# Two raw token tiles in the first wave: layer-norm folded into the PSUM correction of a fused MLP kernel

## The chip, the cores and the metric

The kernel runs on one core of one Trainium2 chip. The metric is device time in microseconds (us) of one execution; lower is better. The number given for a kernel is the median of its runs. Engines are called by the profile's names: PE is TensorE, DVE is VectorE, ACT is ScalarE, POOL is GpSimd, SP is SyncE, which here only starts transfers.

## The reference

A layer-norm without gain or offset, a linear layer with GELU, and a second linear layer, all in bfloat16:

```python
B, S, D, F = 1, 2048, 1024, 3584

def reference(x, w1, b1, w2, b2):
    y = _layernorm(x, axis=-1)               # (x - mean) / sqrt(var + 1e-5)
    h = _gelu(jnp.einsum("bsd,df->bsf", y, w1) + b1)
    return jnp.einsum("bsf,fd->bsd", h, w2) + b2
```

## The kernel before

**Tiling.** The 2048 tokens are 16 tiles of 128 tokens, four tiles to a block of 512. For a block, the first product makes 28 rows (F is 28 x 128). A row is one PSUM bank of 128 x 512 and takes 8 matmuls over the 8 slices `dt` of D; ACT then reads it with GELU and `b1` into `hT_sb` (L432). The second product follows tile by tile, 28 matmuls to a bank (L466); DVE adds `b2` (L477) and SP stores (L482). Blocks run one after another on PE.

**Transposes.** The first product needs x transposed, in `yT_sb` (two buffers, by block number). For blocks 1 to 3 DVE does it out of the PE's way (L355). For block 0 PE does it: `pe_T` (L367) puts 128 x 128 transposes into a PSUM bank and ACT copies them out to `yT_sb` (L385). Tiles 1 to 3 use one bank, `ps_t`, in two groups of four transposes each, so a second group waits until the copy of the first is done.

**The first wave.** As data come in piece by piece, the first 7 rows of block 0 (r = 0 to 6) are not computed 512 tokens at a time but in cells of one tile, one row and one slice: 4 x 7 x 8 = 224 matmuls of 128 columns, in a hand-written order (L508 to L522) in which the transposes of tiles 1 to 3 are inserted at the places of `T_PUTS`. Seven PSUM banks are open at once: five of `ps_1` and two of `ps_2`. Row 7 is the first of full width; it uses `ps_t`, row 8 the bank of row 0, and so on, so row 8 + j waits for the GELU of row j.

**Layer-norm.** DVE takes statistics of a tile in two halves (L264), joins them (L271), POOL raises the variance to the power -0.5 (L268), and DVE normalises (L290). For tiles 0 and 1 only the mean is taken off before the transpose (tile 0 by a mean got early, half of it by ACT, L494; tile 1 at L286). Their factor 1/deviation is put on after the first product: DVE spreads it over the partitions with 16 small transposes (L337), and multiplies columns 0 to 255 of every row of block 0 in PSUM by it before the GELU (`dve_scale`, L423 to L428).

**Order.** Each engine runs its own list in order; a waiting instruction holds all behind it. PE starts with 34 warm-up matmuls on constants, 3 more that wait for tile 0's mean, and 3 after the first transposes (L490). ACT starts the loads of the second half of tile 0 and of tile 1, SP all others: the 8 chunks of w1 that the wave needs (224 KB each, one for each slice), then tiles 2 and 3, `b1`, the rest of w1, x of block 1, w2. DVE's work of later blocks is merged by a small planner (L569 to L584) that only sets the order.

Of the kernel before, what the change touches and what calls it, by code (L numbers as in the profile page):

```python
# [5 lines left out]
ACT = mybir.ActivationFunctionType  # L6
# [5 lines left out]
P = 128  # L12
# [3 lines left out]
K_GROUPS = 2  # L16
# [4 lines left out]
WARM_A = ((34, None), (3, "m4"))  # L21
WARM_B = 3
N_CENTRED = 2
T_PUTS = {0: (None, None, 6), 1: (21, 35), 2: (96, 118), 3: (140, 156)}
NORM = {0: (0, 2, 8), 1: (0, 4, 8), 2: (0, 4, 8)}
GROUPS_0 = (0, 2, 5, 8)
WAVE_ROWS_0 = 6
WAVE_K = (0, 2, 4, 5, 6, 8)
GROUPS_1 = (0, 4, 8)
W1_CHUNK_COLS = (512, 512, 1024, 640)  # L30
N_W2_CHUNKS = 4
SP_FIRST_LOADS = ("x0a", "w0", "w1", "w2", "w3", "w4", "w5", "x2a", "x2b", "w6", "w7", "x3a", "x3b", "b1", "w8")
ACT_FIRST_LOADS = ("x0b", "x1")

T_PE_START = 5.7
T_DVE_START = 16.5
# [54 lines left out]
def bass_standalone__mixer_channel_mlp__prompt_kernel(  # L91
# [22 lines left out]
    nkg = max(1, min(K_GROUPS, DT))  # L114
    KGROUPS = [(h * DT // nkg, (h + 1) * DT // nkg) for h in range(nkg)]
    assert NB1 + NB2 + 1 <= 8 and NB2 == 2
    assert all(c[-1] == DT for c in (*NORM.values(), GROUPS_0, GROUPS_1, WAVE_K))
# [27 lines left out]
    with ExitStack() as es:  # L145
# [19 lines left out]
        half_sb = sb("half_sb", [P, 1], F32)  # L165
        m4_sb = sb("m4_sb", [P, 1], F32)
        rq_sb = sb("rq_sb", [P, N_CENTRED, 32], F32)
        rbc_sb = sb("rbc_sb", [P, N_CENTRED, P], F32)

# [4 lines left out]
        ps_tf = ps_t[:, :, :].bitcast(F32)  # L174

# [83 lines left out]
        pool.op(lambda e: e.memset(b1r_sb[:, :], 0.0), sig="b1z")  # L259
        dve.op(lambda e: e.memset(st_sb[:, :, 12:14], 0.0))  # L260
# [6 lines left out]
        def op_aggr(i):  # L267
            pool.op(lambda e, i=i: e.tensor_tensor(out=rstd_sb[:, i:i + 1], in0=mv_sb[:, i, 1:2],  # L268
                                                   in1=nhalf[:, i:i + 1], op=ALU.pow),
                    waits=[f"mv{i}", "nhalf"], sig=f"rstd{i}")  # L270
            return (lambda e, i=i: e.bn_aggr(mv_sb[:, i, :], st_sb[:, i, :]),  # L271
                    [f"st{i}_0", f"st{i}_1", "eps"], f"mv{i}", 0.33)

        def op_mean0():
            return (lambda e: e.tensor_scalar(out=m4_sb[:, :], in0=st_sb[:, 0, 1:2], scalar1=st_sb[:, 0, 4:5],
                                              scalar2=half_sb[:, :], op0=ALU.add, op1=ALU.add),
                    ["st0_0", "half"], "m4", 0.1)

        def op_norm(i, c0, c1, sig):
            if i == 0:  # L280
                return (lambda e, c0=c0, c1=c1: e.tensor_scalar(
                            out=o_sb[:, 0, c0:c1], in0=x_sb[:, 0, c0:c1], scalar1=4.0,
                            scalar2=m4_sb[:, :], op0=ALU.mult, op1=ALU.subtract),
                        ["m4"], sig, 0.02 + (c1 - c0) * 0.00055)
            if i < N_CENTRED:
                return (lambda e, i=i, c0=c0, c1=c1: e.tensor_scalar(  # L286
                            out=x_sb[:, i, c0:c1], in0=x_sb[:, i, c0:c1], scalar1=mv_sb[:, i, 0:1],
                            scalar2=None, op0=ALU.subtract),
                        [f"mv{i}"], sig, 0.02 + (c1 - c0) * 0.00055)
            return (lambda e, i=i, c0=c0, c1=c1: e.tensor_scalar(  # L290
                        out=x_sb[:, i, c0:c1], in0=x_sb[:, i, c0:c1], scalar1=mv_sb[:, i, 0:1],
                        scalar2=rstd_sb[:, i:i + 1], op0=ALU.subtract, op1=ALU.mult),
                    [f"rstd{i}", f"mv{i}"], sig, 0.02 + (c1 - c0) * 0.00055)
# [3 lines left out]
        def ops_norm(i):  # L297
            cuts = NORM.get(i, (0, DT))
# [27 lines left out]
        def ops_rbc():  # L326
            res = []
            for i in range(N_CENTRED):
                res.append((lambda e, i=i: e.tensor_scalar(out=rq_sb[:, i, :], in0=ones[:, 0:32],
                                                           scalar1=rstd_sb[:, i:i + 1], scalar2=(1.0 if i else 0.25),  # L330
                                                           op0=ALU.mult, op1=ALU.mult),
                            ["ones", f"rstd{i}"], f"rq{i}", 0.1))
            for tq in range(4):
                for q in range(4):
                    src = rq_sb[32 * tq:32 * (tq + 1), :, :]
                    dst = rbc_sb[32 * q:32 * (q + 1), :, 32 * tq:32 * (tq + 1)]
                    res.append((lambda e, src=src, dst=dst: e.transpose(out=dst, in_=src), [f"rq{N_CENTRED - 1}"],  # L337
                                ("rbc" if tq == 3 and q == 3 else None), 0.1))
            return res
# [4 lines left out]
        def ops_T(i):  # L344
            blk, t = divmod(i, TPB)
            waits = [y_ev[i][-1]]
            if blk - 2 in mm1_done:
                waits.append(mm1_done[blk - 2])
            res = []
# [15 lines left out]
        t_banks = [("t", ps_t[:, 0, :]), ("2_0", ps_2b[:, 0, :]), ("t", ps_t[:, 0, :])]  # L365

        def pe_T(i, groups, k):  # L367
            blk, t = divmod(i, TPB)
            j0, j1 = groups[k], groups[k + 1]
            bname, bap = t_banks[k if i == 0 else 0]  # L370
            evs = yT_ev.setdefault(i, [None] * DT)
            for j in range(j0, j1):
# [3 lines left out]
                if j == j0 or y_ev[i][j] != y_ev[i][j - 1]:  # L376
                    waits.append(y_ev[i][j])
                pe.op(lambda e, i=i, j=j, o=(j - j0) * P, bap=bap: e.transpose(  # L378
                    out=bap[:, o:o + P], in_=(x_sb[:, i] if i else o_sb[:, 0])[:, j * P:(j + 1) * P],
                    identity=ident[:, :]),  # L380
# [3 lines left out]
            dst = yT_sb[:, blk % 2, j0:j1, t * P:(t + 1) * P]  # L384
# [23 lines left out]
        def pe_cell(b, r, t0, t1, bank, waits, sig, dts=None, opens=True, closes=True):  # L408
            n0, n1 = t0 * P, t1 * P
            dts = list(range(DT)) if dts is None else list(dts)  # L410
            waits = list(waits)
            for k, dt in enumerate(dts):
                w = (waits if k == 0 else []) + [f"w1c{w1_chunk_of(r, dt)}"]
                w += [yT_ev[b * TPB + t][dt] for t in range(t0, t1)]
                pe.op(lambda e, b=b, r=r, dt=dt, n0=n0, n1=n1, bank=bank: e.matmul(  # L415
                    unit_bank(bank)[:, n0:n1], lhsT=w1_sb[:, dt, r * P:(r + 1) * P], rhs=yT_sb[:, b % 2, dt, n0:n1],
                    start=(opens and dt == 0), stop=(closes and dt == DT - 1)),
                    waits=w, sig=(sig if dt == DT - 1 else None))
            pe_t[0] += len(dts) * _mm_us(n1 - n0)
            if dts[-1] == DT - 1:  # L420
                est[sig] = pe_t[0]

        def dve_scale(r, bank, wait_ev):  # L423
            ap = unit_bank(bank)[:, 0:N_CENTRED * P]
            crit.append((est[wait_ev], (lambda e, ap=ap: e.tensor_tensor(  # L425
                out=ap, in0=ap, in1=rbc_sb[:, :, :].rearrange("p t s -> p (t s)"), op=ALU.mult),
                [wait_ev, "rbc"], f"sc_{r}", 0.35), 0))
            return f"sc_{r}"  # L428
# [11 lines left out]
        def mm1_row(b, r):  # L440
            bank, uw = new_unit()
            sig = f"m1_{b}_{r}"
            pe_cell(b, r, 0, TPB, bank, uw, sig)
            act_gelu(r, 0, TPB, bank, dve_scale(r, bank, sig) if b == 0 else sig, f"g_{b}_{r}")
# [8 lines left out]
        def out_chunk(b, st, c0, c1, region, prev_store):  # L453
# [9 lines left out]
            else:  # L463
                waits.append(bank_gelu[("2", bank)])
            for ft in range(FT):
                pe.op(lambda e, st=st, ft=ft, c0=c0, c1=c1, bank=bank: e.matmul(  # L466
# [21 lines left out]
        def warm(n, gate=None):  # L488
            for _ in range(n):
# [4 lines left out]
        act.op(lambda e: e.activation(out=o_sb[:, 1, 0:HC], in_=x_sb[:, 0, HC:D], func=ACT.Copy, scale=2.0 / HC,  # L494
                                      accum_out=half_sb[:, :]), waits=[x_ev[0][1]], sig="half")
        for n, gate in WARM_A:
            warm(n, gate)
        head = [op_stats(0, 0), op_mean0()] + ops_norm(0) + ln_seq([1], ()) + [op_stats(0, 1), op_aggr(0)]
        for o in head + ln_seq(list(range(2, TPB)), ()) + ops_b1() + ops_rbc():
            dve_put(o)  # L500

        for k in range(2):
            pe_T(0, GROUPS_0, k)
        warm(WARM_B)
        wave = [new_unit() for _ in range(R)]
        r5 = min(R, WAVE_ROWS_0)
        _, ka, kb, kc, kd, _ = WAVE_K
        order = [(0, r, dt) for dt in range(ka) for r in range(r5)]  # L508
        order += [(0, r, dt) for r in range(r5, R) for dt in range(ka)]
        order += [(0, r, dt) for dt in range(ka, kc) for r in range(R)]  # L510
        order += [(1, r, dt) for r in range(R) for dt in range(kb)]
        order += [(0, r, dt) for dt in range(kc, kd) for r in range(R)]
        order += [(1, r, dt) for r in range(R) for dt in range(kb, kd)]
# [114 lines left out]
```

## Time and profile before

| | |
|---|---|
| median of 3 runs | 398.56 us (398.50 to 398.64) |
| span of the profiled execution | 396.9 us |
| PE busy | 394.1 us, 99% of the span |
| DVE, ACT, POOL busy | 152.8, 82.8, 9.7 us |
| L415, first product, all matmuls | 167.4 us (`ps`) and 34.0 us (`ps_t`) |
| L466, second product | 194.2 us |
| DMA | busy in the first 55 us, then near nothing |

The profile is of one execution. Its span, first to last instruction, is 396.9 us; the device time counts what lies around it too, and the median is 1.66 us above the span. A row of the page's groups gives the line, the engine and operation, output and input tiles with their shapes, the count, then busy time, mean duration of one in ns, and idle time of the engine just before them with what ended it. PE's matmuls overlap: a 128-column matmul lasts 219 ns in the records but follows the one before by 56 ns.

### The profile page before, as it was taken

Reading aid. Unit: us, or ns where it says so; the run is one execution under the profiler, and the core shown is the slowest. Engines: PE = TensorE matmul, PEld = TensorE weight load, DVE = VectorE, ACT = ScalarE, POOL = GpSimd, SP = SyncE. Lnnn points to the kernel's source line nnn. Section 1 sums busy time; section 2 is a strip of 40 time slices with the busy share of each in tenths; the row PEclk is TensorE's granted clock in tenths of the full one; section 3 lists DMA queues with packets and bytes.
Section 4 is the critical chain, followed back from the end, with each engine's and each line's share of the span. In section 5 each row is a group of like instructions: output and inputs, shape, how many; then the busy total and the mean of one; then the engine's idle time right before and its main releaser. Section 6 shows DMA issues by size and latency. Waiting matters only on the chain.

```text
span 396.9 us, 4883 instructions
## 1 busy us (share of the span) xinstructions
PE 394.1 (99%) x2116; PEld 191.7 (48%) x2116; DVE 152.8 (38%) x345; ACT 82.8 (21%) x124; POOL 9.7 (2%) x24
## 2 busy tenths in 40 slices
PE   9999999999999999999999999999999999999998
PEld 8944444444444444444444444444444444444447
DVE  5847899989998005988100000001100000001011
ACT  4273430000133442000024433100003334400000
POOL 2101000020002000000000000000000000000000
PEclk9999999999999999999999999999999999999999
DMA  8999940000000000000000000000000000000000
GB/s 286 347 380 384 387 154 13 26 29 13 26 2 0 2 0 1 28 13 26 28 13 0 2 0 2 13 13 28 16 24 15 0 0 2 0 13 28 13 28 26
DMA packets 16924, 23.64 MB, mean 60 GB/s; under 512 B 1672, under 2 KB 10504, under 8 KB 16904
## 3 DMA queue, kind: packets, MB, share of 16 engines
q1 hardware_dynamic: 16616, 22.95, 16.4%
q8 instruction: 16, 0.26, 0.3%
q10 hardware_dynamic: 288, 0.39, 0.3%
q14 instruction: 4, 0.03, 0.0%
HBM read 19.14 MB, written 4.19 MB: 59 GB/s over the span
## 4 chain that ended last, share of the span: by engine, by line
PE 99%; ACT 0%; DVE 0%; issue 0%
PE ps L466 49%; PE ps L415 41%; PE ps_t L415 8%; PE ps L490 1%; PE ps_t L378 0%; ACT yT_sb L385 0%; DVE o_sb L477 0%
## 5 line engine op out<-in xcount | busy, mean ns | idle before, releaser
L466 PE MATMUL ps<-w_sb,hT_sb 128*128 128x512 bf16 (+1 forms) x980 | 194.2, 361 | 0.0
L415 PE MATMUL ps<-yT_sb,w_sb 128*128 128x512 bf16 (+1 forms) x920 | 167.4, 340 | 0.1
L466 PEld LDWEIGHTS ps<-w_sb,hT_sb 128*128 128x128 bf16 x980 | 91.3, 98 | 102.7
L415 PEld LDWEIGHTS ps<-yT_sb,w_sb 128*128 128x128 bf16 x920 | 80.9, 98 | 82.5 <-issue 0.3
L432 ACT ACTIVATE hT_sb<-ps,b_sb 128x512 bf16<-128x512 f32 x94 | 64.0, 688 | 237.2 <-PE ps L415 217.1
L477 DVE TENSOR_TENSOR o_sb<-ps,b_sb 128x512 bf16<-128x512 f32 (+1 forms) x35 | 22.6, 646 | 198.2 <-PE ps L466 198.1
L355 DVE STREAM_TRANSPOSE yT_sb<-x_sb 32x256 bf16<-32x256 bf16 x192 | 83.7, 436 | 26.6 <-PE ps_t L415 23.5
L415 PE MATMUL ps_t<-yT_sb,w_sb 128*128 128x512 bf16 x144 | 34.0, 379 | 0.0
L264 DVE BATCH_NORM_STATS2 st_sb<-x_sb 128x6 f32<-128x512 bf16 x32 | 21.1, 674 | 4.9 <-DMA x_sb<-in_x_dram 4.9
L415 PEld LDWEIGHTS ps_t<-yT_sb,w_sb 128*128 128x128 bf16 x144 | 14.0, 98 | 16.8
L432 ACT ACTIVATE hT_sb<-ps_t,b_sb 128x512 bf16<-128x512 f32 x18 | 12.4, 690 | 17.0 <-PE ps_t L415 14.6
L425 DVE TENSOR_TENSOR ps<-ps,rbc_sb 128x256 f32<-128x256 f32 x24 | 9.7, 426 | 6.1 <-PE ps L415 5.9
L268 POOL TENSOR_TENSOR rstd_sb<-mv_sb,nhalf 128x1 f32<-128x1 f32 x16 | 8.9, 559 | 118.7 <-DVE mv_sb L271 118.7
L290 DVE TENSOR_SCALAR x_sb<-x_sb,mv_sb,rstd_sb 128x1024 bf16<-128x1024 bf16 (+1 forms) x15 | 7.8, 525 | 3.9 <-POOL rstd_sb L268 3.3
L385 ACT COPY yT_sb<-ps_t 128x512 bf16<-128x512 bf16 (+2 forms) x8 | 4.4, 545 | 8.1 <-PE ps_t L378 8.1
L490 PE MATMUL ps<-const-bfloat16-1.0 128*128 128x128 bf16 x40 | 4.6, 302 | 0.8 <-PEq L613 0.8
L490 PEld LDWEIGHTS ps<-const-bfloat16-1.0 128*128 128x128 bf16 x40 | 4.0, 139 | 1.0 <-issue 0.8
L271 DVE BATCH_NORM_AGGREGATE mv_sb<-st_sb 128x2 f32<-128x15 f32 x16 | 3.5, 221 | 1.3
L337 DVE STREAM_TRANSPOSE rbc_sb<-rq_sb 32x64 f32<-32x64 f32 x16 | 3.8, 236 | 0.2
L378 PE MATMUL ps_t<-ident,x_sb 128*128 128x128 bf16 x24 | 2.3, 219 | 0.0
L425 DVE TENSOR_TENSOR ps_t<-ps_t,rbc_sb 128x256 f32<-128x256 f32 x4 | 1.6, 405 | 0.1
L493 ACT ACT_TABLE_LOAD x1 | 1.3, 1283 | 1.7 <-PEq L613 1.7
(24 smaller groups left out, 8.0 us busy)
## 6 DMA issues: line engine op xcount, KB each, us to landing
w_sb<-in_w_dram SPq DMA_DIRECT2D x4, 1792.0 KB, 18.3
out_dram<-o_sb SPq DMA_DIRECT2D x31, 128.0 KB, 1.7
x_sb<-in_x_dram SPq DMA_DIRECT2D x3, 1024.0 KB, 14.1
w_sb<-in_w_dram SPq DMA_DIRECT2D x2, 1024.0 KB, 9.1
w_sb<-in_w_dram SPq DMA_DIRECT2D x1, 2048.0 KB, 15.2
w_sb<-in_w_dram SPq DMA_DIRECT2D x8, 224.0 KB, 4.7
w_sb<-in_w_dram SPq DMA_DIRECT2D x1, 1280.0 KB, 14.7
x_sb<-in_x_dram SPq DMA_DIRECT2D x5, 128.0 KB, 4.6
```

The source lines that it names most:

```text
L264: return (lambda e, i=i, h=h: e.bn_stats(st_sb[:, i, 6 * h:6 * (h + 1)], x_sb[:, i, h * HC:(h + 1) * HC]), [x_ev[i][h]], f"st{i}_{h}", 0.65)
L268: pool.op(lambda e, i=i: e.tensor_tensor(out=rstd_sb[:, i:i + 1], in0=mv_sb[:, i, 1:2], in1=nhalf[:, i:i + 1], op=ALU.pow), waits=[f"mv{i} ...
L290: return (lambda e, i=i, c0=c0, c1=c1: e.tensor_scalar(out=x_sb[:, i, c0:c1], in0=x_sb[:, i, c0:c1], scalar1=mv_sb[:, i, 0:1], scalar2=rst ...
L337: res.append((lambda e, src=src, dst=dst: e.transpose(out=dst, in_=src), [f"rq{N_CENTRED - 1}"], ("rbc" if tq == 3 and q == 3 else None), ...
L355: res.append((lambda e, src=src, dst=dst: e.transpose(out=dst, in_=src), waits, (f"tr{i}" if lastop else None), 0.47))
L385: act.op(lambda e, dst=dst, src=src: e.copy(out=dst, in_=src), waits=[f"tp{i}_{k}"], sig=f"te{i}_{k}")
L415: pe.op(lambda e, b=b, r=r, dt=dt, n0=n0, n1=n1, bank=bank: e.matmul(unit_bank(bank)[:, n0:n1], lhsT=w1_sb[:, dt, r * P:(r + 1) * P], rhs= ...
L425: crit.append((est[wait_ev], (lambda e, ap=ap: e.tensor_tensor(out=ap, in0=ap, in1=rbc_sb[:, :, :].rearrange("p t s -> p (t s)"), op=ALU.m ...
L432: act.op(lambda e, r=r, n0=n0, n1=n1, bank=bank: e.activation(out=hT_sb[:, r, n0:n1], in_=unit_bank(bank)[:, n0:n1], func=ACT.Gelu_apprx_tanh,
L466: pe.op(lambda e, st=st, ft=ft, c0=c0, c1=c1, bank=bank: e.matmul(ps_2[:, bank, 0:c1 - c0], lhsT=hT_sb[:, ft, st * P:(st + 1) * P], rhs=w2 ...
L477: crit.append((est[sig], (lambda e, ob=ob, c0=c0, c1=c1, bank=bank: e.tensor_tensor(out=o_sb[:, ob, c0:c1], in0=ps_2[:, bank, 0:c1 - c0], ...
L490: pe.op(lambda e: e.matmul(ps_1[:, 0, 0:P], lhsT=unit, rhs=unit, start=True, stop=True), waits=[gate] if gate else [])
```

## The change

Tiles 0 and 1 are transposed as they are loaded, with neither mean nor deviation applied, into buffer 1 of `yT_sb`: tile 1 in columns 0 to 127, tile 0 in 128 to 255 (`SLOT_0`). Column 256 of that buffer is set to one. A wave cell of tiles 0 and 1 together has 257 columns (of tile 0 alone 129), so PSUM column 256 of each row gathers the sum of its weights over D. ACT copies these sums out (`act_cs`), and the cells of tile 2, which lie on columns 256 to 383, then add onto that column.

When a row of the wave is complete, DVE multiplies columns 0 to 256 by a row vector that holds 1/deviation of each token (and 1), and adds the weight sum times a second row vector that holds -mean/deviation (and -1, which takes the sum off column 256 again). The two vectors are made by DVE as columns, turned by four 32 x 32 transposes, stored by ACT's queue to device memory (2 KB) and loaded back to all 128 partitions (256 KB), the second transfer waiting for the first on ACT. For rows 7 on, DVE makes normalised tiles 0 and 1 in buffer 0 of `yT_sb` from the raw ones with the same vectors (`ops_fix`, four operations on 128 x 1024), so the scaling of rows 7 to 27 in PSUM goes. Row 7 is done in two halves, tiles 2 and 3 first.

Tile 1's load moves from ACT's queue to third place on SP's. There are 24 warm-up matmuls, and none after. The transposes of tiles 2 and 3 stand at new places in the wave, which has 28 cells of 128 or 129 columns for tiles 0 and 1, 42 of 257, and 112 of 128 for tiles 2 and 3. Rows 8 to 27, blocks 1 to 3, the second product and the stores keep their instructions.

```diff
-WARM_A = ((34, None), (3, "m4"))
-WARM_B = 3
+WARM = 24
+N_RAW = 2
+RC = N_RAW * P
+SLOT_0 = (1, 0, 2, 3)
-SP_FIRST_LOADS = ("x0a", "w0", "w1", "w2", "w3", "w4", "w5", "x2a", "x2b", "w6", "w7", "x3a", "x3b", "b1", "w8")
-ACT_FIRST_LOADS = ("x0b", "x1")
+SP_FIRST_LOADS = ("x0a", "w0", "x1", "w1", "w2", "w3", "x2a", "x2b", "w4", "w5", "w6", "w7", "x3a", "x3b", "b1", "w8")
+ACT_FIRST_LOADS = ("x0b",)
...
+        pool.op(lambda e: e.memset(yT_sb[:, 1, :, RC:RC + 1], 1.0), sig="rone")
...
+        def op_nmr(i):
+            return (lambda e, i=i: e.tensor_scalar(out=nmr_ap[i], in0=mv_sb[:, i, 0:1], scalar1=rstd_ap[i],
+                                                   scalar2=-1.0, op0=ALU.mult, op1=ALU.mult),
+                    [f"rstd{i}", f"mv{i}"], f"nmr{i}", 0.1)
+        def ops_rvt():
+            return [(lambda e, q=q: e.transpose(out=rvt_sb[:, 32 * q:32 * (q + 1)], in_=rv_sb[32 * q:32 * (q + 1), :]),
+                     ["nmr0", "nmr1"], ("rvt" if q == 3 else None), 0.18) for q in range(4)]
...
+        def ops_fix(i):
+            s0, s1 = SLOT_0[i] * P, (SLOT_0[i] + 1) * P
+            return [(lambda e: e.tensor_tensor(out=tmp_sb, in0=yT_sb[:, 1, :, s0:s1], in1=row_bc(0, s0, s1),
+                                               op=ALU.mult),
+                     ["rows", f"te{i}_{len(GROUPS_1) - 2}", f"te{i}_0"] + ([f"fx{i + 1}"] if i == 0 else []), f"fm{i}", 1.1),
+                    (lambda e: e.tensor_tensor(out=yT_sb[:, 0, :, s0:s1], in0=tmp_sb, in1=row_bc(1, s0, s1),
+                                               op=ALU.add),
+                     [f"fm{i}"], f"fx{i}", 1.1)]
...
-        for o in head + ln_seq(list(range(2, TPB)), ()) + ops_b1() + ops_rbc():
+        for o in ln_seq([0], ()) + ln_seq([1], ()) + [op_nmr(0), op_nmr(1)] + ops_rvt() + ln_seq([2], ()):
             dve_put(o)
...
+        for o in stats3 + ops_b1() + norm3 + ops_fix(1) + ops_fix(0):
+            dve_put(o)
...
+        def act_cs(banks, r0, r1, flip):
+            src = banks[:, :, RC]
+            act.op(lambda e: e.copy(out=cs_sb[:, r0:r1], in_=src), waits=[f"cw_{r}" for r in range(r0, r1)],
+                   sig=f"cs_{r0}")
...
+        def ops_corr(r):
+            ap = unit_bank(wave[r][0])[:, 0:RC + 1]
+            return [(lambda e: e.tensor_tensor(out=ap, in0=ap, in1=row_sb[:, 0, :], op=ALU.mult),
+                     [f"m1_0_{r}", "rows", "row1"], f"sa_{r}", 0.43),
+                    (lambda e: e.scalar_tensor_tensor(out=ap, in0=row_sb[:, 1, :], scalar=cs_ap[r], in1=ap,
+                                                      op0=ALU.mult, op1=ALU.add),
+                     [f"sa_{r}", cs_ev[r]], f"sb_{r}", 0.43)]
+
+        pe_T(0, 0, "t")
+        pe_T(0, 1, "2_0")
+        t0_cells(range(r5), (0,))
+        pe_T(1, 0, "t")
+        t0_cells(range(r5), (1,))
+        pe_T(1, 1, "2_0")
+        act.op(lambda e: e.dma_start(rows_d, rvt_sb[0:2 * N_RAW, :]), waits=["rvt"],
+               sig="rvd", sem="d_rvd", inc=16)
+        act.op(lambda e: e.dma_start(row_sb[:, :, 0:RC],
+                                     rows_d.rearrange("(k t) s -> k (t s)", k=2).partition_broadcast(P)),
+               waits=["rvd", "row1"], sig="rows", sem="d_rows", inc=16)
+        t1_cells(range(r5), (0, 1))
+        raw_both(range(r5), (2,))
+        t0_cells(range(r5, R), (0, 1))
+        t1_cells(range(r5, R), (0, 1))
+        raw_both(range(r5, R), (2,))
+        raw_both(range(R), range(3, DT - 1))
+        pe_T(2, 0, "t")
+        raw_both(range(NB1), (DT - 1,))
+        act_cs(ps_1, 0, NB1, False)
+        raw_both(range(NB1, R), (DT - 1,))
+        act_cs(ps_2, NB1, R, True)
+        pe_T(2, 1, "t")
+        h = DT // 2
+        wave_cells(2, range(R), range(h))
+        wave_cells(2, range(4), range(h, DT))
+        pe_T(3, 0, "t")
+        wave_cells(2, range(4, R), range(h, DT))
+        r4 = R // 2 + 1
+        wave_cells(3, range(2), range(h))
+        pe_T(3, 1, "t")
+        wave_cells(3, range(2, r4), range(h))
+        wave_cells(3, range(r4), range(h, DT))
+        wave_cells(3, range(r4, R), range(DT))
+        for o in corr:
+            dve_put(o)
...
-                mm1_row(b, r)
+                mm1_row(b, r, ((TPB // 2, TPB), (0, TPB // 2)) if b == 0 and r == r0 else ((0, TPB),))
```

## The prediction

> **What bounds the kernel now.** I read the chain that ended last first: it is PE from end to end.
>
> ```profile
> PE 99%; ACT 0%; DVE 0%; issue 0%
> ```
>
> So only what moves PE's stream counts, and the change touches its first 20 us alone. The same chain, cut to the first 22 us (start, length, what; x is the number of instructions), shows that stretch:
>
> ```profile
> 0.82 4.26 PE ps L490 x37
> 5.08 0.30 PE ps_t L378 x2
> 5.38 0.02 issue
> 5.40 0.38 ACT yT_sb L385
> 5.78 0.14 issue
> 5.92 0.49 PE ps L415 x6
> ...
> 16.37 3.80 PE ps L415 x68
> ```
>
> The wave's first cell starts at 5.92, after warm-up, two transposes and their copy. In the groups by shape of the first 20 us, the cells have no idle time to speak of:
>
> ```profile
> L415 PE MATMUL ps<-yT_sb,w_sb 128*128 128x128 bf16 x224 | 13.9, 219 | 0.1
> ```
>
> The timeline of PE and ACT shows what one group of four transposes costs, and where row 7 begins (20.00):
>
> ```profile
> 14.86 0.39 PE L378 MATMUL ps_t<-ident,x_sb 128*128 128x128 bf16 x4
> 15.29 0.58 ACT L385 COPY yT_sb<-ps_t 128x512 bf16<-128x512 bf16 x1 [0.86 <-PE ps_t L378]
> ...
> 20.00 1.89 PE L415 MATMUL ps_t<-yT_sb,w_sb 128*128 128x512 bf16 x8
> ```
>
> The copy starts 0.43 after the first transpose and takes 0.585; PE can use it 0.06 later (the group at 7.26 lets PE go on at 8.32 in the same way). So from first transpose to usable data: **1.07 us**. Before, 16 to 22 cells (0.056 each, 0.9 to 1.2 us) stand behind each group, and PE never waits.
>
> PE's spacing is at half rate at first. In windows of 1 us (length, then busy time and count of PE):
>
> ```profile
> 2.00:3.00 1.00, 1.00 (x12) 1.00 (x10) 0.00 (x0) 0.98 (x1) 0.00 (x0) 1.00 1.07 303
> ...
> 6.00:7.00 1.00, 1.00 (x20) 1.00 (x20) 0.86 (x3) 0.54 (x2) 0.22 (x1) 1.00 1.01 367
> ```
>
> The counts include neighbours in flight; by the starts it is one per 107 ns until about 5.3 us, and one per 56 ns after, though the clock column says 1.00 in both.
>
> **PE's path in the changed kernel**, step by step, in us from the span's start. 128 columns cost 0.056 and 512 cost 0.216 (L415), so on that line 257 columns cost 0.110.
>
> - 24 warm-ups at 0.107 from 0.82 end at 3.43; the first half of tile 0 is there (issued 0.78, 2.4 to landing). Eight transposes at 0.107: to 4.29. The copy of the first two (0.37) is usable at 4.33.
> - Chunk 0 of w1 lands by 4.5 (issued 1.22, 3.3 to landing). Six cells at 0.108: 4.53 to 5.18.
> - Tile 1 now stands behind chunk 0 on SP. The bytes ahead are the same as before, when it landed at 4.9 (issued 1.21, 3.7), so I take 5.0 to 5.1: no wait. Four transposes from 5.18 cross the change of rate and end at 5.51; the copy is usable at 6.36. Meanwhile PE has six cells and four transposes (to 6.07), then waits **0.29**.
> - 12 cells, 6 wide ones, 5 of row 6, 28 wide ones: 0.67 + 0.66 + 0.33 + 3.07, to 11.09. The chunks of slices 2 to 6 are due at 7.03, 8.02, 8.79, 9.56, 10.32. By the bytes ahead of them they land at 6.7, 7.3, 8.6, 9.2, 9.8 (landings before of the loads with as many bytes ahead): hidden by 0.2 at least.
> - Tile 2: DVE does the statistics of tile 1 from 5.1 (aggregate 1.39 after the first, as 8.89 to 10.28 in the rows below), waits for POOL (0.89 from aggregate to the next operation), makes the vectors (0.3) and turns them (four transposes, at most 0.25 each as at L337; I take 0.2): 8.4. Then tile 2: aggregate 9.8, normalise 10.67, first piece done 11.08. PE starts its transposes at 11.14, **0.05** late.
> - Seven wide cells behind them end at 12.13, but the single bank is free at 11.14 + 1.07 = 12.21: wait **0.08**. Second group to 12.43, 28 + 16 cells to 14.88, tile 3's first group (normalised at 14.1) to 15.10, 12 cells to 15.77; its data come at 15.95: wait **0.18**. 8 cells to 16.40, second group to 16.62, 8 cells to 17.07; data at 16.40 + 1.07 = 17.47: wait **0.40**. 40 cells: 19.70.
>
> ```profile
> 8.89 1.29 DVE L264 BATCH_NORM_STATS2 st_sb<-x_sb 128x6 f32<-128x512 bf16 x2 [0.68 <-DMA x_sb<-in_x_dram]
> 10.28 0.22 DVE L271 BATCH_NORM_AGGREGATE mv_sb<-st_sb 128x2 f32<-128x15 f32 x1
> 11.16 0.73 DVE L290 TENSOR_SCALAR x_sb<-x_sb,mv_sb,rstd_sb 128x512 bf16<-128x512 bf16 x2 [0.67 <-POOL rstd_sb L268]
> ```
>
> So the start comes 1.4 us earlier, but six cells and twelve transposes of it run at half rate, and four short covers give 0.71 back besides the 0.29. Row 7 starts at 19.70 instead of 20.00; its two halves cost 16 x 0.109 against 8 x 0.216: +0.02. **Sum: -0.28 us.**
>
> **What must stay hidden.**
>
> - *ACT's queue.* The vectors are ready at 8.4. ACT starts the store, then waits for its landing before it can start the load, and behind that wait stands the copy of tile 2, due at 11.14 + 0.43 = 11.57, for which PE waits. The issue takes 0.45. The store's landing time L has no row; the bounds are 1.7 (out stores, on quiet queues) and 3.7 (tile 1 on ACT's queue, 256 KB). It is a small store, but among loads: I take 2.2. ACT is free at 11.1, spare 0.46; PE waits for all of L over 2.66.
> - *The load of the vectors*, 256 KB like tile 1: 2.6 (tile 0's half, on the same queue) to 3.7; I take 3.7: landed 14.35. It also puts 256 KB ahead of chunk 8 (landed 16.6 before, +0.7), needed at 19.7.
> - *`ops_fix`* has no row. The nearest are L425, 256 columns 0.43, and L477, 512 columns 0.69: 1.05 ns a column, so 1.23 for 1024 and 1.3 with the wait between dependent ones. Below, 0.55 (1024 columns at L290); above, 1.7 (four of L425's 0.43). Four take 5.2: 14.35 to 19.55. Row 7's second half needs them at 20.57.
> - *The correction of the wave rows*: two operations of 0.43 for one of 0.34 spacing, 0.92 to the first row's end, 0.82 for each more. Row 0 at 20.47, its GELU (0.69) usable at 21.27; row 8 needs the bank at 21.45: spare **0.18**. Later rows gain 0.9 each (PE 1.73 a row, DVE 0.82).
> - The removed scaling of rows 7 to 27 and the 16 transposes of L337 were off the path; `act_cs` and the memsets lie beside PE's cells.
>
> Against the execution's own span, 396.9 - 0.28 = 396.6; with the 1.66 that the median lies above it, **398.3 us**.
>
> **The rivals.**
>
> 1. *ACT's queue holds the copy* (slower). At L = 3.7 ACT is free at 12.6, tile 2's data come at 13.25 instead of 12.21 (+1.04), and the vectors' later landing makes row 8 wait 0.28: 399.6. It turns the sign from L = 2.94 on. For it: the DMA engines are busy 0.99 of the time from 9 to 12 us. Against it: 2 KB only. [...] No trace here shows a small store between loads.
> 2. *The rate changes late* (slower). Half rate lasted 4.5 us from the first matmul. The new head has three more transposes and fewer plain matmuls in that stretch. If transposes do not count for it, and the 4.5 us began anew with the first cell at 4.4, the half rate would last to 8.9: half of 3.6 us lost, less the 0.34 of waits it covers, +1.4: 399.7. Against it: the five transposes and 0.37 us of gaps before 5.3 did no harm before. [...]
> 3. *The covers suffice* (faster). If copies come back sooner than 1.07, all waits fall: -1.0 more, 397.3. Against it: all six copies of this shape in the wave take 0.585.
> 4. *DVE's chain is too long* (slower). With 1.7 an operation, the upper bound, `ops_fix` ends at 21.4, row 7 waits 0.84 and row 8 another 0.84: 400.0. It decides from 1.3 on, as the spare is 0.18 over four. Against it: L425 and L477 give the same slope.
>
> **How the numbers follow.** About 0.2% (0.8 us) is what a measurement of this kernel can tell from no change: below 397.8 is faster, above 399.4 slower. Forecast 50% (its own range 397.8 to 398.9; 3 points of it faster, 3 slower), rival 1 19% (half of it beyond 399.4), rival 2 10%, rival 3 16%, rival 4 5%. Faster 3 + 16 = 0.19; slower 3 + 10 + 10 + 5 = 0.28; the rest, 0.53, the same. The range reaches to rivals 1, 2 and 3 and leaves out rival 4 and their far ends: 397.3 to 399.8.
>
> **What would show it.** First cell of L410 near 4.5 instead of 5.92; PE idle near 6.1, and before tile 3's data 0.2 and 0.4; row 7's first matmul near 19.7. If ACT's first copy of tile 2 starts well after its transposes, rival 1 holds; if cells follow at 0.107 after 5.4, rival 2; if `ps` of row 8 waits for GELU by more than 0.3, rival 4. I am wrong if row 7 starts before 19.2 or after 20.8.

## The result and the profile after

| | before | after |
|---|---|---|
| median | 398.53 us (4 runs, 398.22 to 398.64) | **403.86 us** (4 runs, 402.45 to 405.17) |
| ratio, 95% interval | | 1.0135 [1.0108, 1.0162] |
| span of the profiled execution | 396.9 us | 403.3 us |
| row 7's first matmul | 20.00 | 20.93 |
| PE busy | 394.1 us | 393.6 us |

The changed kernel is 1.35% slower; the forecast was 398.3 us, no change. The profiled execution of after took 404.65 us, of which 403.3 is span, so there are 6.4 us of span to find.

The chain that ended last, as shares by engine, was 99% PE before. Now the page has:

```profile
PE 92%; DMA 3%; DVE 2%; issue 1%; ACT 0%; POOL 0%; DVEq 0%
```

The same chain, cut to the first 40 us (start, length, what):

```profile
8.61 3.71 DMA rows_d<-rvt_sb
...
12.34 7.47 DMA row_sb<-rows_d
...
19.83 1.24 DVE o_sb L331
...
21.09 1.24 DVE yT_sb L334
...
24.75 0.43 DVE ps L554
...
25.73 0.70 ACT hT_sb L419
```

The head of the kernel is no longer set by PE but by the way of the two row vectors: 3.71 us to store 2 KB, 7.47 us to load it back to all partitions, then DVE's four fix operations, then the first correction and its GELU. PE's own timeline from 19 us on, with the idle time before a row and its releaser in brackets, shows who waits for it:

```profile
18.81 2.29 PE L410 MATMUL ps<-yT_sb,w_sb 128*128 128x128 bf16 x38
20.93 1.04 PE L410 MATMUL ps_t<-yT_sb,w_sb 128*128 128x256 bf16 x8
24.98 1.03 PE L410 MATMUL ps_t<-yT_sb,w_sb 128*128 128x256 bf16 x8 [3.01 <-DVE yT_sb L334]
26.80 4.56 PE L410 MATMUL ps<-yT_sb,w_sb 128*128 128x512 bf16 x13 [0.79 <-ACT hT_sb L419]
```

Row 7's second half waits 3.01 us for the last fix operation, row 8 another 0.79 for row 0's GELU. There is a third loss that no wait shows. In windows (length, then busy time and count of PE, PEld, DVE, ACT, POOL, then the granted clock, DMA share, GB/s):

```profile
23.19:26.60 3.41, 1.03 (x8) 0.82 (x10) 3.31 (x7) 0.69 (x2) 0.00 (x0) 1.00 1.06 367
26.60:30.01 3.41, 3.21 (x8) 1.18 (x8) 3.27 (x9) 2.75 (x4) 0.00 (x0) 0.50 1.06 382
30.01:33.00 2.99, 2.99 (x15) 1.35 (x14) 2.20 (x5) 2.79 (x5) 0.00 (x0) 1.00 1.05 386
```

After the waits PE is busy again, but the clock column falls to 0.50 and 8 matmuls pass in 3.41 us, where the next 2.99 us hold 15. From 26.80 to 30.01 at half rate costs 1.6 us.

So the 6.4 us are: row 7 late by 0.93, its second half 3.01, row 8 0.79, half rate 1.6; sum 6.33. The split between the last two is rough. Row 8's first two weight loads stand just behind the end of the GELU, and its first matmul has no record:

```profile
26.47 0.11 PEld L410 LDWEIGHTS ps<-yT_sb,w_sb 128*128 128x128 bf16 x2 [0.74 <-ACT hT_sb L419]
```

Row 8 thus began near 26.49, the wait for the GELU was about 0.5, and the stretch at half rate cost about 1.7.

### The profile page after: what moved, and what is told of

Same layout as the page of the kernel before. It is cut to its first block, busy times and chain, and to the rows that moved or that the text cites. A ratio compares the mean times of both kernels' runs of the same rounds, so it can differ in the third digit from the quotient of the medians.

```text
span 403.3 us, 4733 instructions
## 1 busy us (share of the span) xinstructions
PE 393.6 (98%) x2032; PEld 191.3 (47%) x2066; DVE 148.8 (37%) x319; ACT 82.7 (21%) x123; POOL 9.7 (2%) x27
## 4 chain that ended last, share of the span: by engine, by line
PE 92%; DMA 3%; DVE 2%; issue 1%; ACT 0%; POOL 0%; DVEq 0%
PE ps L464 48%; PE ps L410 37%; PE ps_t L410 7%; DMA row_sb<-rows_d 2%; DMA rows_d<-rvt_sb 1%; DMA x_sb<-in_x_dram 1%; DVE o_sb L331 1%; DVE st_sb L268 1%; DVE yT_sb L334 0%; DVE rvt_sb L284 0%; ACT hT_sb L419 0%; POOL rv_sb L272 0%; DVE ps L556 0%; DVE mv_sb L275 0%; DVE ps L554 0%
## 5 line engine op out<-in xcount | busy, mean ns | idle before, releaser
L410 PE MATMUL ps<-yT_sb,w_sb 128*128 128x512 bf16 (+3 forms) x860 | 168.2, 351 | 2.4 <-ACT hT_sb L419 0.8
L410 PE MATMUL ps_t<-yT_sb,w_sb 128*128 128x512 bf16 (+1 forms) x151 | 34.0, 368 | 3.1 <-DVE yT_sb L334 3.0
L272 POOL TENSOR_TENSOR rstd_sb<-mv_sb,nhalf 128x1 f32<-128x1 f32 x14 | 7.7, 549 | 115.5 <-DVE mv_sb L275 115.5
L385 ACT COPY yT_sb<-ps_t 128x512 bf16<-128x512 bf16 (+1 forms) x6 | 3.3, 550 | 10.4 <-PE ps_t L379 5.3
L331 DVE TENSOR_TENSOR o_sb<-yT_sb,row_sb 128x1024 f32<-128x1024 bf16 x2 | 2.4, 1224 | 5.5 <-DMA row_sb<-rows_d 5.5
L488 PE MATMUL ps<-const-bfloat16-1.0 128*128 128x128 bf16 x24 | 2.7, 309 | 0.8 <-PEq L674 0.8
L556 DVE SCALAR_TENSOR_TENSOR ps<-row_sb,cs_sb,ps 128x257 f32<-128x257 f32 x7 | 3.4, 490 | 0.2
L554 DVE TENSOR_TENSOR ps<-ps,row_sb 128x257 f32<-128x257 f32 x7 | 3.0, 426 | 0.0
L488 PEld LDWEIGHTS ps<-const-bfloat16-1.0 128*128 128x128 bf16 x24 | 2.5, 143 | 0.8 <-issue 0.8
L334 DVE TENSOR_TENSOR yT_sb<-o_sb,row_sb 128x1024 bf16<-128x1024 f32 x2 | 2.4, 1224 | 0.1
```

What stands on the lines that cost most here:

```text
L272: pool.op(lambda e, i=i: e.tensor_tensor(out=rstd_ap[i], in0=mv_sb[:, i, 1:2], in1=nhalf[:, i:i + 1], op=ALU.pow), waits=[f"mv{i}", "nhalf ...
L331: return [(lambda e: e.tensor_tensor(out=tmp_sb, in0=yT_sb[:, 1, :, s0:s1], in1=row_bc(0, s0, s1), op=ALU.mult), ["rows", f"te{i}_{len(GRO ...
L410: pe.op(lambda e: e.matmul(unit_bank(bank)[:, n0:n1], lhsT=w1_sb[:, dt, r * P:(r + 1) * P], rhs=yT_sb[:, buf, dt, n0:n1], start=start, sto ...
L488: pe.op(lambda e: e.matmul(ps_1[:, 0, 0:P], lhsT=unit, rhs=unit, start=True, stop=True), waits=[gate] if gate else [])
L556: (lambda e: e.scalar_tensor_tensor(out=ap, in0=row_sb[:, 1, :], scalar=cs_ap[r], in1=ap, op0=ALU.mult, op1=ALU.add), [f"sa_{r}", cs_ev[r] ...
```

## The experiments

Twelve kernels ran, each beside the kernel before. Ratios are to that kernel's runs on the same chip, with the 95% interval.

| | edit | median us | ratio |
|---|---|---|---|
| e1 | both vector transfers on SP, ahead of chunk 8 | 400.57 | 1.0051 [1.0036, 1.0066] |
| e2 | chunk 8 and later held until the vectors are there | 399.35 | 1.0027 [1.0015, 1.0038] |
| e3 | load issued later on ACT | 405.79 | 1.0195 [1.0178, 1.0212] |
| e4 | after, with filler matmuls ahead of row 7 | 403.28 | 1.0137 [1.0096, 1.0177] |
| e5 | e1 and e2 together | 399.76 | 1.0028 [1.0016, 1.0041] |
| e6 | e5, tile 1 back on ACT's queue | 398.83 | 1.0010 [1.0000, 1.0020] |
| e7 | before, PE waits 4.4 us ahead of row 7 | 405.11 | 1.0160 [1.0145, 1.0175] |
| e8 | before, PE waits 1.3 us there | 399.65 | 1.0028 [1.0017, 1.0039] |
| e9 | e5, plain matmuls in the head | 399.32 | 1.0024 [1.0016, 1.0033] |
| e10 | e6, a smaller filler, other covers | 399.08 | 1.0018 [1.0009, 1.0026] |
| e11 | before, 24 warm-ups in place of 34 | 399.27 | 1.0029 [1.0017, 1.0041] |
| e12 | e10, short chunk 8 first, half the fix on POOL | 399.22 | 1.0023 [1.0012, 1.0033] |

### Is it the load's place, or what runs beside it (e1, e2, e3)?

e1 takes both transfers from ACT and puts them into SP's list, behind `b1` and ahead of chunk 8:

```diff
-SP_FIRST_LOADS = (... "x3a", "x3b", "b1", "w8")
+SP_FIRST_LOADS = (... "x3a", "x3b", "b1", "rows", "w8")
-        act.op(lambda e: e.dma_start(rows_d, rvt_sb[0:2 * N_RAW, :]), waits=["rvt"], ...
-        act.op(lambda e: e.dma_start(row_sb[:, :, 0:RC], ...
+            elif item == "rows":
+                sp.op(lambda e: e.dma_start(rows_d, rvt_sb[0:2 * N_RAW, :]), waits=["rvt"], ...
+                sp.op(lambda e: e.dma_start(row_sb[:, :, 0:RC], ...
```

> The changed kernel with both transfers of the vectors moved from ACT's queue to SP's, between b1 and the first big chunk of w1 (chunk 8), so no big load is started until the vectors' load has been. Theory (the vectors come late because both transfers stand behind big loads in the DMA engines): the load lands by about 14 instead of 19.8, PE's waits for ops_fix (3.0) and for row 0's GELU (0.8) go, the half rate after 26.6 goes, and ACT's copy of tile 2 is not held (0.5): 399.2 us, 398.6 to 399.9. Rival (a store to device memory and a load of one 2 KB piece to 128 partitions are slow by themselves): load still 6 to 8 us, 403 to 404 us.

Measured: 400.57 us, above the range expected. The store takes 2.78 us (9.35 to 12.13) and the load 5.12 (12.14 to 17.26), so it lands well after the 14 expected: chunk 8 was issued on the same queue 0.45 behind it, and chunk 9 after that. PE waits 0.71 for the fix and 0.47 for the GELU, and the clock stays at 1.00:

```profile
22.44 1.03 PE L416 MATMUL ps_t<-yT_sb,w_sb 128*128 128x256 bf16 x8 [0.71 <-DVE yT_sb L340]
23.94 8.81 PE L416 MATMUL ps<-yT_sb,w_sb 128*128 128x512 bf16 x40 [0.47 <-ACT hT_sb L425]
```

e2 leaves the transfers on ACT, and holds the loads behind them instead:

```diff
             dma(w1_sb[:, j0:j1, a:b], w1v[:, j0:j1, a:b], f"w1c{ci}", (j1 - j0) * P * (b - a) * 2,
+                waits=(["rows"] if ci == DT else ()))
```

> The changed kernel with chunk 8 of w1, and so all loads behind it on SP, held until the vectors' load has landed; both transfers stay on ACT's queue. Theory (behind big loads): store 2 to 3 us, load 2 to 3.5 us, landed by 14.5, waits of PE before row 8 under 0.5 us together, no half rate: 399.5 us, 398.8 to 400.3, and with the first run of this set it tells what ACT's blocked queue costs (0 to 0.5). Rival (slow by themselves): 403 to 404, and 1 us more where chunk 8 is then late for row 7.

Measured: 399.35 us (10 runs). The list of DMA issues (KB each, us from issue to landing) has for the load in e2:

```profile
row_sb<-rows_d ACTq DMA_DIRECT2D x1, 256.0 KB, 3.2
```

and for the same instruction in after:

```profile
row_sb<-rows_d ACTq DMA_DIRECT2D x1, 256.0 KB, 7.5
```

What differs is the other traffic while it is under way. The window from 12 to 16 us (the last two columns are DMA share and GB/s), first e2, then after:

```profile
12.00:16.00 4.00, 3.16 (x52) 2.85 (x51) 2.28 (x7) 1.30 (x4) 0.55 (x1) 1.00 0.20 66
```

```profile
12.00:16.00 4.00, 3.44 (x56) 3.10 (x54) 1.95 (x6) 1.30 (x4) 0.55 (x1) 1.00 1.06 364
```

With DMA nearly idle in that window (share 0.20), the load takes 3.2 us; with the later chunks of w1 filling the engines (1.06), 7.5. In e2 no wait in rows 7 or 8 is left and the clock stays at 1.00 in the profiled execution; two of the ten runs, both at 400.7, show a mean clock of 0.996. That takes back 4.5 of the 5.3 us. What remains, 0.9, is row 7's start: 21.02 against 20.00 before. The store takes 3.84 us even here, though chunk 8 and all loads behind it are held; it still holds tile 2's copy on ACT, and PE waits 0.84 for it:

```profile
13.46 0.40 PE L380 MATMUL ps_t<-ident,x_sb 128*128 128x128 bf16 x4 [0.84 <-ACT yT_sb L386]
...
21.02 1.92 PE L411 MATMUL ps_t<-yT_sb,w_sb 128*128 128x256 bf16 x16
```

e3 puts the load behind the first copy of tile 2 on ACT, so that ACT's queue holds no copy:

```diff
-        act.op(lambda e: e.dma_start(row_sb[:, :, 0:RC], ...
         pe_T(2, 0, "t")
...
         pe_T(2, 1, "t")
+        act.op(lambda e: e.dma_start(row_sb[:, :, 0:RC], ...
```

> The changed kernel with the load of the vectors started on ACT behind the second copy of tile 2, so that ACT's queue holds no copy; it starts about 1.1 us later. Theory (only the landing of the vectors counts, the held copy of 0.5 us lies inside the wait it makes): the wave ends 0.5 earlier, row 8 about 1 us later than in the changed kernel: 404.5 us, 403.5 to 406. Rival (my rival 1: the held copy is what costs): 403.3 or less.

Measured: 405.79 us, slower than after. PE's timeline:

```profile
26.05 1.72 PE L410 MATMUL ps_t<-yT_sb,w_sb 128*128 128x256 bf16 x8 [4.38 <-DVE yT_sb L334]
```

The held copy is gone: tile 2's two groups of transposes start 1.06 us apart (12.05 and 13.11), where they are 1.72 apart in after (11.69 and 13.41), so the held copy costs 0.66 us. Row 7 starts at 20.63, only 0.30 earlier than in after, because chunk 1 of w1 landed 0.35 later in this execution (6.68 against 6.33). But the load, started at 13.61, takes 7.27 and lands at 20.88; the wait grows to 4.38. A later start of the load costs more than the copy is worth. e1 to e3 together: the landing of the vectors decides most of the loss, and the traffic beside the load decides the landing (the load took 7.47 us in after, 5.12 in e1, 3.2 in e2).

### What does a wait of PE cost by itself (e4, e7, e8)?

e4 puts 14 matmuls of 512 columns into `ps_t` ahead of row 7 in after, to keep PE busy:

```diff
+        for k in range(14):
+            pe.op(lambda e: e.matmul(ps_tf[:, 0, :], lhsT=ident[:, :], rhs=w1_sb[:, 0, 0:512], start=True, stop=True),
+                  waits=[bank_read["t"]])
```

> The changed kernel with 14 matmuls of 512 columns on data already there (3.0 us, results overwritten by row 7) put between the wave and row 7, in the place of the time that PE waits for ops_fix in row 7. All else is the same and the vectors come as late. Theory (the idle 3 us brings PE's rate down to half from 26.6 to 30.0, which costs 1.6 us): row 8 starts at the same time within 0.5, no half rate: 402.3 us, 401.3 to 403.2. Rival (the half rate is no result of the wait): 403.9 us, with the clock at 0.996 still.

Measured: 403.28 us (402.52 to 406.33), which leaves the price of the half rate in after open: the interval is too wide. Three of the four runs show a mean clock of 1.0, where three of after's four show 0.996; that fits the theory, and four runs each are too few for more. The profiled execution, the longest of the four, shows something else. Timeline of PE, then windows:

```profile
16.16 0.60 PE L379 MATMUL ps_t<-ident,x_sb 128*128 128x128 bf16 x4 [2.02 <-ACT yT_sb L385]
```

```profile
12.44:15.86 3.42, 1.56 (x15) 0.93 (x13) 2.95 (x8) 0.34 (x1) 0.58 (x2) 1.00 1.08 362
15.86:19.27 3.41, 3.10 (x30) 3.11 (x31) 0.11 (x1) 0.96 (x4) 0.00 (x0) 0.50 1.08 370
```

Here the store took 4.84 us (10.23 to 15.07) where it took 3.71 in after, though no instruction ahead of it is changed; ACT held tile 2's copy for it, PE waited 2.02, and the next 3.41 us went at half rate. What differs in this execution is when it started: tile 1 landed at 6.74 instead of 5.11, so the vectors were ready 1.6 us later, and chunks 8 and 9 (issued at 9.33 and 9.78) had now been issued ahead of the store, where in after it went out before chunk 8 (9.11). Whether that made it slower was not tried; the store's landing is not a fixed number.

e7 and e8 measure a wait in the kernel before, where no other part of the change is present. PE waits for POOL memsets between the wave and row 7, four of them in e7, one in e8:

```diff
+        junk = sb("junk", [P, 1000], F32)
+        for k in range(4):
+            pool.op(lambda e: e.memset(junk[:, :], 0.0), waits=[f"junk{k - 1}" if k else f"m1_0_{R - 1}"], sig=f"junk{k}")
+        pe.op(None, waits=["junk3"])
```

> The kernel before, with PE made to wait between the wave and row 7 for four memsets of POOL in a chain that starts when the wave ends (about 3.5 us, 3 to 5); nothing else is changed. Theory (PE idle for more than about half of one of the 3.41 us windows brings half rate for the next): the wait and 1.0 to 1.7 us more: with 3.5 us of wait 403.2 us, clock 0.996. Rival (only the wait itself costs): 398.4 and the wait, 401.9, clock 1.0.

> As e7 with one memset (about 1.0 us of wait, 0.8 to 1.4). Both theories: the time before and the wait alone, 399.4 us, clock 1.0; a lower clock here would mean that a wait of 1 us is enough.

Measured: e8 399.65 us (399.46 to 399.75), 1.1 more than before for a wait of 1.28 (row 7's first matmul has no record, so the wait is some 0.2 shorter). e7 405.11 us, 6.6 more for a wait of 4.42. PE's timeline in e8, and the windows of e7:

```profile
21.64 1.67 PE L416 MATMUL ps_t<-yT_sb,w_sb 128*128 128x512 bf16 x7 [1.28 <-POOL junk L542]
```

```profile
20.00:24.19 4.19, 0.24 (x5) 0.06 (x2) 1.35 (x5) 3.55 (x7) 3.71 (x4) 1.00 1.06 374
24.19:27.60 3.41, 2.94 (x7) 1.20 (x9) 0.00 (x0) 0.00 (x0) 0.01 (x1) 0.50 1.06 376
27.60:30.00 2.40, 2.40 (x12) 1.08 (x11) 0.86 (x2) 0.69 (x1) 0.00 (x0) 1.00 1.05 387
```

The short wait costs itself. The long one costs itself and then a stretch of 3.41 us at half rate, with 7 matmuls where the full rate, at 0.216 us each, has some 16: in this execution 4.42 + 2.94/2 = 5.9, which is its span over that of before, 402.8 - 396.9. The mean clock of the run was 0.996; one such stretch is 3.41/2 of 403 us, 0.4%. The three other runs of e7 had 0.992, which would be two such stretches; no profile shows the second.

### What is left once the vectors come in time (e5, e6, e9, e11)?

e5 joins the edits of e1 and e2. e6 also takes tile 1 off SP:

```diff
-SP_FIRST_LOADS = ("x0a", "w0", "x1", "w1", ... "rows", "w8")
-ACT_FIRST_LOADS = ("x0b",)
+SP_FIRST_LOADS = ("x0a", "w0", "w1", ... "rows", "w8")
+ACT_FIRST_LOADS = ("x0b", "x1")
```

> The changed kernel with both transfers of the vectors on SP's queue as in e1 and the big loads held until they have landed as in e2. Theory (load slowed by the big loads behind or beside it: 3.2 us in e2 against 5.1 in e1 and 7.5 in the changed kernel; ACT's queue held costs PE 0.5 to 0.8 in e2): landed by 15.5, no wait of PE on tile 2's copy over 0.2, row 7 near 20.3, no wait in row 7, under 0.4 in row 8: 398.9 us, 398.4 to 399.4. Rival (the queue the load stands on sets its time, the loads behind it do not): load over 4.5 us again and 400.0 or more.

> As e5, and tile 1's load back on ACT's queue, as before the change. Theory (third place on SP makes tile 1 land at 5.0 to 6.7, and as late a start of all that follows): tile 1 lands by 4.9, row 7 starts 0.3 to 0.8 earlier than in e5, the runs spread less; row 8 then waits up to 0.5 for row 0's GELU: 398.5 us, 398.0 to 398.9. Rival (bytes ahead are the same, the place does not matter): the same as e5 within 0.2.

Measured: e5 399.76 us, e6 **398.83** (10 runs, 398.47 to 400.47). In both the load takes 3.2 us and no wait in rows 7 and 8 is left. Tile 1 lands at 5.85 in e5 and at 5.04 in e6; over all the profiles it lands at 5.03 to 6.74 in the seven kernels that load it on SP, and at 4.89 to 5.15 in the seven that load it on ACT. Its place is all that differs between e5 and e6, so it costs the 0.9 us between them, as far as their intervals tell them apart. About half of that is that four of e5's eight runs lie at 400.2 or above, and one of e6's ten; without these the medians are 399.3 and 398.8. e6 is the best version of the change, and its interval reaches down to no change.

The profiled executions of both show the prediction's second rival. e5's windows around the change of rate:

```profile
9.00:10.00 1.00, 1.00 (x7) 0.73 (x5) 0.95 (x4) 0.00 (x0) 0.00 (x0) 1.00 1.05 398
10.00:11.00 1.00, 1.00 (x13) 0.86 (x12) 0.85 (x3) 0.00 (x0) 0.00 (x0) 1.00 0.93 306
```

The cells are spaced at half rate until 10.1 us, with no wait of PE from 6.46 on, and row 7 starts at 22.10; in e6 it is 10.04 and 21.91. e6's profiled run (400.47) is 1.1 us above the next of its runs, so this probably comes in some executions only, and in e6 seldom. After, with the same head as e5, went to full rate at 6.12.

e9 adds 6 and 4 plain matmuls on constants to e5, ahead of tile 1's two groups of transposes. e11 takes only the warm-ups from the kernel before:

```diff
+        fill_pe(6, ps_tf[:, 0, 0:P], "te0_0")
+        fill_pe(4, ps_2[:, 0, 0:P], "te0_1")
```

```diff
-WARM_A = ((34, None), (3, "m4"))
+WARM_A = ((24, None), (3, "m4"))
```

> e5 with 6 plain matmuls on constants before tile 1's first transposes and 4 before its second (into banks that nobody reads yet), where PE waited for tile 1 and for chunk 1 in e5. Theory (half of e5's runs are at 400.2 to 400.7 because the full rate came at 10.1 us instead of about 6: the head is mostly transposes and waits): the full rate comes before 7 us in every profile, no run over 399.8, median 399.3. Rival (when the full rate comes is luck of the window's phase, or the slow half has another cause): the median stays at 399.8, with runs over 400.2.

> The kernel before with 24 instead of 34 warm-up matmuls, the 3 gated ones kept; PE idles about 1.1 us before them. Theory (fewer plain matmuls in the head make the full rate late): some or all runs 1.0 to 1.7 us above 398.5, or cells at 107 ns spacing after 6 us in the profile. Rival (the transposes and 27 warm-ups are enough): 398.5 within 0.2.

Measured: e9 399.32 us, and full rate by about 4.4 in its profile; but row 7, at 20.64, waits 0.34 for chunk 8, which this kernel holds back. Two of its eleven runs still lie just above 400, so a late rate is not shown to be gone from all. e11 399.27 us. Its windows:

```profile
7.00:8.00 1.00, 1.00 (x14) 1.00 (x12) 1.00 (x3) 0.48 (x1) 0.72 (x1) 1.00 1.07 354
8.00:9.00 1.00, 1.00 (x22) 1.00 (x19) 0.66 (x3) 0.30 (x1) 0.49 (x1) 1.00 1.07 385
```

With 24 warm-ups in place of 34, the kernel before goes to full rate near 7.8 us instead of 5.3, and row 7 starts at 21.02 instead of 20.00. Its first cell is only 0.22 late (6.14 against 5.92). Fewer warm-ups alone make it 0.8 us slower: these idle-looking matmuls were on the path through the rate they bring (107 ns a matmul until 7.8 us here, until 5.3 with 34).

### Does a mended version beat the kernel before (e10, e12)?

e10 is e6 with 3 and 2 plain matmuls in the head, tile 3's transposes moved up so that more cells stand behind them, and row 0's correction ahead of the last fix operation:

```diff
+        fill_pe(3, ps_tf[:, 0, 0:P], "te0_0")
+        fill_pe(2, ps_2[:, 0, 0:P], "te0_1")
-        wave_cells(2, range(4), range(h, DT))
+        wave_cells(2, range(5), range(h, DT))
...
-        for o in corr:
+        for o in corr[:2] + fix0[1:] + corr[2:]:
```

> A version meant to beat both kernels: e6, with 3 and 2 plain matmuls in the head, tile 3's transposes put earlier so that 20 and 24 cells stand behind their groups instead of 12 and 8, and the correction of row 0 put before the last operation of ops_fix. Theory (what is left in e6 is the 0.2 and 0.4 us before tile 3's data, the late full rate in some runs, and row 0's GELU as the last to be ready): row 7 near 19.7, row 8 waits under 0.3: 398.2 us, 397.8 to 398.7. Rival (DVE's chain from the vectors' landing at 15.1, 6.7 us to row 0's GELU, sets row 8 whatever PE does): row 7 earlier, row 8 no earlier than 21.8, 398.6 to 399.0.

Measured: 399.08 us. The wave ends at 19.83, but

```profile
20.77 1.92 PE L417 MATMUL ps_t<-yT_sb,w_sb 128*128 128x256 bf16 x16 [0.94 <-DMA w_sb<-in_w_dram]
```

row 7 now waits for chunk 8, which the hold has delayed: the cure of the load has a price of its own, which neither the theory nor its rival had. e12 sends a short chunk 8 (rows 7 and 8 only) ahead of the load and gives tile 0's fix to POOL:

```diff
-W1_CHUNK_COLS = (512, 512, 1024, 640)
+W1_CHUNK_COLS = (256, 768, 1024, 640)
-                waits=(["rows"] if ci == DT else ()))
+                waits=(["rows"] if ci == DT + 1 else ()))
...
+        for o in ops_fix(0):
+            pool.op(o[0], waits=o[1], sig=o[2])
```

> Takes out of the version before the two things that seemed left in it: chunk 8 goes ahead of the load, cut to 256 columns, so that only later chunks are held until the vectors have landed; and tile 0's two fix operations go to POOL, so that DVE has two of them and then the corrections. Theory (the 0.94 us wait for chunk 8 was all that stood between that version's wave, which ended at 19.83 us, and row 7): row 7 starts near 19.8, no wait before rows 7 and 8 above 0.3, 398.2 us (397.8 to 398.8), at or a little below the kernel before. Rival (the two fix operations on POOL take over 2.4 us each, more than DVE's 1.24 beside it, or the short chunk ahead of the load delays it past 16 us): row 7's second half or row 8 waits 0.5 to 1.5 us, 398.8 to 400. If a full rate that comes late decides instead, row 7 starts after 20.8 with no wait in the trace, 399.5.

Measured: 399.22 us; row 7 starts at 19.75, the earliest of all, and its second half waits 0.79:

```profile
15.31 3.19 POOL L341 TENSOR_TENSOR tmp_sb<-yT_sb,row_sb 128x1024 f32<-128x1024 bf16 x1 [1.65 <-DMA row_sb<-rows_d]
18.57 2.86 POOL L344 TENSOR_TENSOR yT_sb<-tmp_sb,row_sb 128x1024 bf16<-128x1024 f32 x1
```

The expectation's rival came true: POOL takes 3.19 and 2.86 us for what DVE does in 1.24. No version beat the kernel before; all of e6, e9, e10 and e12 lie within 0.3% of it, above it.

## Why the prediction was wrong

- **The load of the vectors is the term that failed.** The text put its bounds at 2.6 to 3.7 us, from loads of 128 and 256 KB in the first 5 us, and took 3.7. It took 7.47. The DMA engines were not idle in the bounding row (tile 1, share 0.80), but only 256 KB had been issued ahead of it. The load of the vectors started at 12.34 with chunks 8 to 10 of w1, 4 MB, issued on SP and none landed; the share was 1.03 while it ran. The same paragraph had the 256 KB delay chunk 8, but not the other way round, and the 0.99 share from 9 to 12 us was weighed for the store alone. e2 shows that way: 3.2 us without these chunks. No rival had a slower load, and none a time above 400.0.
- **The store** was taken at 2.2, at most 3.7; it took 3.71, and 2.57 (e9) to 4.84 (e4) in the runs. So rival 1 came true as far as ACT's queue goes: at 3.7 it had tile 2's data at 13.25, and PE went on at 13.41. Its 399.6 was far too low because it kept the load at 3.7. In the eight profiles other than e4 that show its landing, it came 0.4 to 1.0 us after that of tile 3's second half, issued before it; whether it waits for such loads was not tried.
- **With the right two terms the prediction's own steps give the waits.** Landing at 19.81 plus four operations of 1.26 is 24.85; row 7's second half started at 24.98. The fix operations (1.23 and 1.3 foretold, 1.24 and 1.26 measured) and the correction (0.82 a row, measured 0.86) were right. So the place was that of rival 4, DVE's chain, but its cause was the DMA ahead of it.
- **Half rate after a wait was missed.** No sum of the prediction had a wait cost more than its length. Here it is 1.6 to 1.7 us more, by the windows of after; e7 shows the effect without the change (a wait of 4.42, then 3.41 at half rate), and e8 that a short wait, 1.28, did not bring it.
- **Row 7's start** was foretold at 19.70 and came at 20.93. Two steps make the difference. Chunk 1 of w1 landed at 6.33, where the working had it in time: the second six cells began at 6.38 and tile 2's transposes at 11.69 instead of 11.14. The estimate by bytes ahead failed here, since chunk 1 had the same bytes ahead before, and landed at 5.45. And ACT was held by the store until 12.34, as rival 1 has it: tile 2's copy started at 12.77, 0.65 later than its transposes at 11.69 would allow. In the timeline of the head:

```profile
6.38 0.51 PE L410 MATMUL ps<-yT_sb,w_sb 128*128 128x129 bf16 x6 [0.52 <-DMA w_sb<-in_w_dram]
```

```profile
11.69 0.39 PE L379 MATMUL ps_t<-ident,x_sb 128*128 128x128 bf16 x4
...
12.34 0.39 ACTq L568 DMA_DIRECT2D row_sb<-rows_d  x1
12.77 0.59 ACT L385 COPY yT_sb<-ps_t 128x512 bf16<-128x512 bf16 x1 [5.04 <-PE ps L410]
...
13.41 0.40 PE L379 MATMUL ps_t<-ident,x_sb 128*128 128x128 bf16 x4 [0.56 <-ACT yT_sb L385]
```

- **What held:** the first cell at 4.53 (4.60; partly luck, since tile 0 landed 0.2 later than the working had it and chunk 0 of w1 0.25 earlier), tile 1's transposes at 5.18 (5.22), the vectors ready at 8.4 (8.58), the waits before tile 3's data (0.18 and 0.40 foretold, the same in PE's weight loads). Rival 2, the late rate, is real but not in after's profile (6.12); e5 (10.1), e6 (10.04) and e11 (7.8) show it. That transposes do not count for the rate was an assumption; no run shows it. Rival 3 is out: the copies kept their 0.59.
- **Open:** after's four runs lie 2.7 us apart, those of before 0.4. Three of after's show a mean clock of 0.996, as one stretch at half rate gives, and the fourth (403.06) shows 1.0, so the half rate does not come in every execution. Unequal landings of tile 1, store and load, as between after and e4, would spread the runs, but only one execution of each kernel was profiled.

## What to carry to other kernels

A small transfer that sits on the critical path must be priced beside the traffic that will run with it, not by a row of the same size that had little issued ahead of it: here 7.5 us against 3.2, and the cure, holding later loads, has to be checked for who needs those loads next. A wait of PE of some 2 us or more (here 2.02 was enough once, and 1.28 was not) is to be priced with the half rate that can follow it (3.41 us in after, e4 and e7), and warm-up matmuls with the rate that they bring (here full rate at 5.3 us with 34, at 7.8 with 24). A step that DMA, DVE and ACT must finish in a row before PE can go on needs slack for its worst landing, not for its likeliest (here the store took 2.57 to 4.84 us).

## What the runs showed of the hardware

- **The changes of rate lay multiples of 3.413 us apart.** In the trace of after, full rate is on record from 6.12 us for 20.48 us (6 x 3.413), then half rate for 3.413 (26.60 to 30.01). In e7 the warm-ups go to full rate near 3.7 us by their spacing, and half rate came at 24.19, 20.5 later; it lasted 3.41 there (24.19 to 27.60) and in e4 (15.86 to 19.27). In e4 the change to full rate fell in a gap of PE, between 4.96 and 6.79: 15.86 less 3 x 3.413 is 5.62, which fits, but no matmul shows it.
- **Idleness in part of the 3.41 us before it was enough.** PE was busy for 1.03 of the 3.41 us before the half rate in after, and for 1.56 in e4, where the gap of 2.02 began in that stretch and ran 0.3 us past its end. The waits of 0.71 and 0.47 in e1, and of 1.28 in e8, brought none. Waits between 1.28 and 2.02 were not tried, and the half of a window that e7's expectation names was an assumption.
- **The head can miss the change to full rate.** With a head of transposes, short cells and waits it came at 6.12 in after, but at 10.1 in e5 and by 4.3 in e2, whose heads are the same. The clock column of e5's windows shows 1.00 even from 7 to 8 us, with 12 matmuls there, where e9's at full rate has 17; only the matmuls' spacing shows the change.
- **POOL beside DVE.** In e12 DVE's second fix operation took 3.05 us while POOL ran its own, against 1.24 in after; its first, which also ran beside POOL, took 1.23.
